# Second FFN of a fused attention and FFN kernel: SyncE's transfers in written order, token loads behind the last reads of their buffers, partial sums loaded two blocks ahead

## The chip, the core and the metric

One NeuronCore of a Trainium2 chip runs the whole program. Its engines work side by side, each in order: TensorE (PE) multiplies, VectorE (DVE), ScalarE (ACT) and GpSimd (POOL) work on tiles, SyncE (SP) issues most DMA transfers, ScalarE some. The metric is the device time of one execution in microseconds; the median of three runs is compared.

## What is computed

State attention, a first gated FFN (moe) and a second one (moe2). The change lies in the second, on 4352 tokens of 512 numbers (8 x 544), with 1536 hidden numbers:

```python
def _moe2_ref(x, w_gate, w_val, w_out):
    gate = 1.0 / (1.0 + np.exp(-(x @ w_gate)))
    val = x @ w_val
    return (gate * val @ w_out).astype(np.float32)
```

The weights arrive as 64-bit numbers. The kernel keeps each factor as a pair of rounded parts, high and low, and multiplies high with high, high with low and low with high.

## The kernel before, the second FFN

The 34 blocks of 128 tokens are cut in five groups, `c` = 0 to 4, of 7, 7, 7, 7 and 6 blocks. The 1536 hidden columns are cut in three passes, `ps`. So there are 15 steps `(ps, c)`, the passes outside. A step has two halves, `gate_val(ps, c, q, ...)` with q = 0 and 1, each for 256 hidden columns of the gate (a = 0) and of the value (a = 1). A half forms its 2 x 2 blocks of output (hidden by tokens, n = 448 or 384 tokens) by seven products of the Strassen-Winograd kind and not by eight: fourteen "products" of six matmuls for a = 0 and 1 together. They go to PSUM banks psA (k = 1, 6, 5, 3), psB (k = 7, 4) and psC (k = 2). psA is one running sum: after k = 1, 6 and 5 ScalarE copies it out (`keep_`, the rows u<-psA and s<-psA), and the next product into that bank waits for the copy. VectorE's `finish` adds and multiplies, ScalarE takes the sigmoid, and the result, split in two parts, is the tile p.

`down(ps, c)` multiplies p with the output weights, block by block, 12 matmuls of 512 columns each, into one of three po banks. It is put into the next step, behind the first three products of its first half (`between`). In the first pass the block is copied to a tile `ob` (VectorE and ScalarE by turns) and stored to `part_d[0]`; in the second and third pass the earlier partial sum is loaded to a tile `pr`, VectorE adds (line 1026), and the sum is stored to `part_d[1]` or the output. `pr` and `ob` have two buffers each; the load for block s + 1 is written in block s, ahead of its add.

Token tiles: the seven right-hand factors of group c + 1 ("tokens", tiles y) are made while group c is multiplied. `next_tokens` holds the list: four loads `get(kb, h)` of 448 KB (tile yf, three buffers; the fourth comes from ScalarE's queue), four sums per kb (`diff`, tiles yt), and fourteen `part`s, each a copy on ScalarE and a subtraction on VectorE (line 590, one step later). The fourth load of a group takes the buffer of its second, which is read early; the loads (0,1) and (1,0) of the next group wait for the very last reads of this group, the parts (5,1) and (6,1), which fall into the down.

Meanwhile `next_weights` makes the weights of the next pass: loads and stores on ScalarE's queue (`raw2`, `wd`), bit operations on ScalarE and VectorE (`conv`), sums on GpSimd (`comb`), splits on ScalarE and GpSimd (`put`). `load_wt(ps, q)` loads the two weight tiles `wt[q, 0]` and `wt[q, 1]` of a half, 1792 KB each; `load_wo` the output weights.

Order: within `tc.manual_schedule` ScalarE, VectorE and GpSimd run what the code writes, in that order. TensorE's order is written too. SyncE is not in the list: its transfers are placed by the tile framework's scheduler. A planner decides where tokens and weights stand: `clock` counts steps (a product 1.2 us, half a down block 1.35 us) and a budget of VectorE time; `begin` runs what is due (`later`), and `fill`, behind each product or each half block, takes list entries from `prep` and `tokens` while the entry's condition holds. `at(k)` is true k products behind the middle of a step. For the first entries, parts (0,0) and (0,1) and the first four sums, the condition is `begun`, three products behind the three loads, which stand together at the head of the step.

## Time and profile before

| | us |
|---|---|
| median of 3 runs | 1444.26 (1442.82 to 1445.51) |
| the profiled execution | 1441.65 |
| its span | 1439.8 |
| TensorE busy in the span | 1350.2 (94%) |
| VectorE, ScalarE, GpSimd busy | 958.2 (67%), 747.9 (52%), 279.8 (19%) |
| the second FFN's matmuls, first start to last end | 630.40 to 1431.02 |

From 630 us on TensorE is busy in nine tenths or more of nearly every slice of the page, and its granted clock reads 9 tenths or more in each. Its matmuls are pipelined, so the starts of groups that follow each other tell more than the busy time: where the next group starts later than the work before it takes, TensorE has lost time. The profile's "idle before" names who released it.

### The profile page before, as it was taken

The page shows a single profiled execution, that of the slowest core. Times are in us where ns is not written, and L with a number is a line of the kernel's source. Part 1 is how long each engine was busy: PE and PEld are TensorE (multiplying, and loading weights), DVE is VectorE, ACT ScalarE, POOL GpSimd, SP SyncE. Part 2 cuts the span into 40 slices and gives each one's busy share as a digit, 9 for nine tenths or more (in the row PEclk, how much of TensorE's full clock was granted, in tenths as well). Part 3 has the DMA queues.
Part 4 walks back from the last instruction along what each step waited for, and adds up shares of the span by engine and source line. Part 5 has one row for each costly group of instructions (what it writes and reads, how often), then busy time and mean ns, then how long its engine had stood idle before and what let it go on. Part 6 is the DMA issues. An engine that isn't in the chain of part 4 may idle for free. (4 is left out here: it accounts for less than half of the span.)

```text
span 1439.8 us, 19119 instructions
## 1 busy us (share of the span) xinstructions
PE 1350.2 (94%) x6560; PEld 1148.4 (80%) x6560; DVE 958.2 (67%) x1639; ACT 747.9 (52%) x1480; POOL 279.8 (19%) x255
## 2 busy tenths in 40 slices
PE   4667999999999999999999999899999999999997
PEld 3446877778777777898888998888978988988996
DVE  7789866664574575628578687678768557556543
ACT  6766557665455456535556555545545434434421
POOL 2253023323243234001122210221211000000000
PEclk9699999999999999999999999999999999999999
DMA  9767836764345244383343358464463662242232
GB/s 276 241 184 206 231 112 209 223 210 116 138 137 159 90 147 157 122 330 114 134 160 115 135 183 313 162 214 143 163 209 122 249 241 92 88 128 87 74 103 73
DMA packets 169129, 237.19 MB, mean 165 GB/s; under 512 B 46920, under 2 KB 111944, under 8 KB 166984
## 3 DMA queue, kind: packets, MB, share of 16 engines
q1 hardware_dynamic: 130536, 163.15, 36.2%
q10 hardware_dynamic: 37344, 63.39, 12.5%
q0 software_dynamic: 1152, 9.44, 1.7%
q8 instruction: 51, 0.84, 0.2%
q14 instruction: 46, 0.38, 0.1%
HBM read 150.99 MB, written 84.93 MB: 164 GB/s over the span
## 5 line engine op out<-in xcount | busy, mean ns | idle before, releaser
L912 PE MATMUL psA<-y,wt 128*128 128x448 f32 (+1 forms) x1440 | 307.9, 362 | 12.2 <-ACT u L61 11.7
L912 PEld LDWEIGHTS psA<-y,wt 128*128 128x128 f32 x1440 | 268.1, 189 | 34.1 <-ACT u L61 14.9
L1010 PE MATMUL po<-wo,p 128*128 128x512 f32 x1224 | 283.6, 392 | 4.2 <-DVE ob L1026 3.8
L1010 PEld LDWEIGHTS po<-wo,p 128*128 128x128 f32 x1224 | 229.9, 189 | 54.2 <-DVE ob L1026 5.5
L112 PE MATMUL pab<-aT,swh 128*128 128x512 f32 x512 | 146.1, 408 | 21.4 <-ACT asb L61 9.8
L912 PE MATMUL psB<-y,wt 128*128 128x448 f32 (+1 forms) x720 | 161.6, 360 | 0.0
L912 PEld LDWEIGHTS psB<-y,wt 128*128 128x128 f32 x720 | 134.2, 189 | 8.6
L66 POOL TENSOR_TENSOR o<-m,o 128x256 fp32r<-128x256 f32 x72 | 61.4, 853 | 384.6 <-ACT o L61 362.4
L112 PE MATMUL py<-u,wp 128*128 128x512 f32 (+1 forms) x576 | 131.6, 380 | 2.3 <-DVE u L66 2.0
L112 PEld LDWEIGHTS pab<-aT,swh 128*128 128x128 f32 x512 | 95.2, 193 | 45.2 <-ACT asb L61 11.6
L112 PEld LDWEIGHTS py<-u,wp 128*128 128x128 f32 x576 | 103.4, 188 | 28.4 <-issue 5.7
L61 ACT ACTIVATE u<-psA 128x448 f32<-128x448 f32 (+1 forms) x120 | 63.4, 529 | 118.2 <-PE psA L912 96.3
L66 POOL TENSOR_TENSOR swh<-swf,swh 128x512 fp32r<-128x512 f32 x64 | 93.4, 1463 | 159.3 <-ACT swh L61 132.1
L434 DVE TENSOR_TENSOR asb<-asb,pab 128x512 f32<-128x512 f32 (+1 forms) x72 | 47.1, 653 | 97.1 <-PE pab L115 90.2
L61 ACT ACTIVATE p<-sg 128x448 fp32r<-128x448 f32 (+1 forms) x120 | 67.9, 565 | 82.1 <-DVE sg L948 72.8
L61 ACT ACTIVATE y<-yf 128x448 fp32r<-128x448 f32 (+1 forms) x120 | 62.7, 557 | 69.9 <-DMA yf<-yd 67.3
L590 DVE TENSOR_TENSOR y<-yf,y 128x448 fp32r<-128x448 f32 (+1 forms) x112 | 67.5, 626 | 45.8 <-ACT y L61 45.8
L1026 DVE TENSOR_TENSOR ob<-po,pr 128x512 f32<-128x512 f32 x68 | 46.7, 687 | 59.8 <-DMA pr<-part 36.2
L98 DVE SCALAR_TENSOR_TENSOR m<-raw,m 128x512 uint32<-128x512 uint32 (+1 forms) x116 | 81.7, 706 | 2.8
L101 DVE CUSTOM_DVE_ANT_0 m<-m,r 128x1024 uint16<-128x1024 uint16 (+1 forms) x116 | 75.1, 648 | 10.3 <-ACT u L61 0.5
L115 PE MATMUL pab<-aT,swh 128*128 128x512 f32 x256 | 81.4, 400 | 0.2
L93 DVE TENSOR_SCALAR m<-m 128x512 f32<-128x512 f32 (+1 forms) x116 | 53.0, 457 | 42.9 <-ACT m L88 42.5
(119 smaller groups left out, 2090.8 us busy)
## 6 DMA issues: line engine op xcount, KB each, us to landing
raw<-in_moe_w SPq DMA_DIRECT2D x48, 512.0 KB, 5.0
wt<-wd SPq DMA_DIRECT2D x12, 1792.0 KB, 7.4
part<-ob SPq DMA_DIRECT2D x68, 256.0 KB, 2.8
pr<-part SPq DMA_DIRECT2D x68, 256.0 KB, 3.7
yf<-yd SPq DMA_DIRECT2D x37, 448.0 KB, 4.3
swd<-swst ACTq DMA_DIRECT2D x32, 512.0 KB, 3.6
swf<-swd SPq DMA_DIRECT2D x128, 128.0 KB, 3.3
wd<-o ACTq DMA_DIRECT2D x56, 256.0 KB, 2.3
```

The lines of the kernel that those rows point to most:

```text
L61: return nc.scalar.activation(out=o, in_=i, func=AF.Copy)
L66: (sub or nc.vector).tensor_tensor(out=lo, in0=src, in1=hi.bitcast(F32), op=ALU.subtract)
L93: nc.vector.tensor_scalar_max(m, m, 2.0**-15)
L98: nc.vector.scalar_tensor_tensor(out=mu, in0=hi, scalar=0xC0000000, in1=mu, op0=ALU.bitwise_and, op1=ALU.bitwise_or)
L101: nc.vector.tensor_tensor(out=m.bitcast(I32), in0=m.bitcast(I32), in1=r, op=ALU.add)
L112: nc.tensor.matmul(o, w[i], xx[k], start=n == 0 and i + k == 0, stop=False)
L115: nc.tensor.matmul(o, w[1 - late], xx[late], start=False, stop=n == len(pairs) - 1)
L434: p2["dve"] = nc.vector.tensor_tensor(out=asb[:, :n], in0=asb[:, :n], in1=pab[1][:, :n], op=ALU.mult)
L590: nc.vector.tensor_tensor(out=o, in0=x0, in1=x1, op=ALU.subtract)
L912: nc.tensor.matmul(o, w[:, i, kb * P : (kb + 1) * P], xx[kb][h], start=start, stop=i == 1 and kb == 1, skip_group_check=True,)
L1010: nc.tensor.matmul(o, pt[j][i][:, s * P : (s + 1) * P], wot[j][:, h], start=j == js[0] and i + h == 0, stop=j == js[-1] and i == 1,)
L1026: nc.vector.tensor_tensor(out=ob, in0=o, in1=pr[s], op=ALU.add)
```

## The change

1. SyncE joins the engines whose order is written. The transfers are therefore placed by hand: at the stage's head wt of the first half, the token loads, wt of the second half, the output weights; at a pass change `wt[1, 0]` before the down and `wt[1, 1]` behind it.
2. Of the three SyncE token loads only (0,0) stays at the head of a step; (0,1) and (1,0) become list entries behind part (6,1) of the group before, run one step later. `get` notes when a load should have landed by the planner (2.5 us plus 2.2 us each, one after the other); the first parts and sums wait for that (`here`). Part (0,1) now stands behind the four sums.
3. `load_pr` asks for block s + 2, two blocks ahead of the add; blocks 0 and 1 are asked for at the head of the step. `ob` and `pr` become one tile with four buffers, and the add is in place.
4. In `next_weights` a sum no longer stands in the same or the next entry to the split that reads it.

```diff
--- before.py
+++ after.py
@@ -668,7 +668,7 @@
 
 
 
-        clock = {"now": 0, "us": 0.0, "vector": 0.0, "prep": 10.0}
+        clock = {"now": 0, "us": 0.0, "vector": 0.0, "prep": 10.0, "load": 0.0}
         due = {}
         tokens = []
         prep = []
@@ -705,6 +705,9 @@
                         fn()
             while tokens and clock["vector"] > 0.5 and act < 2 and tokens[0][0]():
                 _, is_split, fn = tokens.pop(0)
+                if is_split is None:
+                    later(1, 0.0, fn)
+                    continue
                 if is_split:
                     act += 1
                 else:
@@ -718,8 +721,8 @@
         def new_p(j):
             pt[j] = [c2.tile([P, 896], F32R, name=f"p{j % JQ}_{i}") for i in range(2)]
 
-        def load_wt(ps, q):
-            for a in range(2):
+        def load_wt(ps, q, both=(0, 1)):
+            for a in both:
                 t = c2.tile([P, 7, 2, 256], F32R, name=f"wt{q}{a}")
                 nc.sync.dma_start(
                     out=t.rearrange("p o i f -> p (o i f)").bitcast(F32),
@@ -746,9 +749,11 @@
             ready.difference_update([(c, o, kb) for o in range(7) for kb in range(2)])
             raw = {}
             t = {}
+            landed = {}
 
             def get(kb, h, queue=nc.sync):
                 raw[kb, h] = y_raw(c, kb, h, c2, 448, queue)
+                clock["load"] = landed[kb, h] = max(clock["load"], clock["us"] + 2.5) + 2.2
 
             def diffs(kb):
                 (b11, b12), (b21, b22) = raw[kb, 0], raw[kb, 1]
@@ -777,13 +782,21 @@
                         later(2, 0.0, lambda: get(1, 1, nc.scalar))
                 return fn
 
+            def here(*need):
+                return lambda: all(k in landed and clock["us"] >= landed[k] for k in need)
+
             get(0, 0)
-            get(0, 1)
-            get(1, 0)
-            begun = clock["now"] + 3
-            first = at(1) if clock["now"] == 0 else lambda: clock["now"] > begun
-            out = [(first, True, part(0, 0)), (first, True, part(0, 1))]
-            out += [(first, False, lambda i=i: diff(0, i)) for i in range(4)]
+            if clock["now"] == 0:
+                get(0, 1)
+                get(1, 0)
+                first = [at(1)] * 3
+                out = []
+            else:
+                first = [here((0, 0)), here((0, 0), (0, 1)), here((1, 0))]
+                out = [(lambda: True, None, lambda k=k: get(*k)) for k in ((0, 1), (1, 0))]
+            out += [(first[0], True, part(0, 0))]
+            out += [(first[1], False, lambda i=i: diff(0, i)) for i in range(4)]
+            out += [(first[2], True, part(0, 1))]
             out += [(at(2), True, part(o, 0)) for o in (4, 5)]
             out += [(at(5), True, part(1, 0)), (at(8), True, part(4, 1))]
             out += [(at(8), True, part(o, 0)) for o in (2, 3)]
@@ -859,23 +872,20 @@
                     m["s"] = m[22]
 
                 def s2():
-                    put(d[5], 21)
+                    comb(21, 11, 21)
                     comb("s", "s", 11)
-
-                def s4():
-                    put(d[0], 11)
-                    comb("s", 12, "s")
 
                 get(21)
                 get(22)
                 step(s1)
+                get(11)
                 step(lambda: put(d[3], "s"))
-                get(11)
-                step(lambda: comb(21, 11, 21))
                 step(s2)
+                step(lambda: put(d[0], 11))
+                step(lambda: put(d[5], 21))
+                get(12)
                 step(lambda: put(d[4], "s"))
-                get(12)
-                step(s4)
+                step(lambda: comb("s", 12, "s"))
                 step(lambda: put(d[1], 12))
                 step(lambda: put(d[6], "s"))
 
@@ -991,16 +1001,15 @@
             ):
                 step(a, k)
 
+        pr = {}
+
+        def load_pr(ps, c, s):
+            if ps and s < blocks[c]:
+                pr[s] = c2.tile([P, DM], F32, name="ob", bufs=4)
+                nc.sync.dma_start(out=pr[s], in_=part_d[ps - 1][first[c] + s])
+
         def down(ps, c):
             js = range(ps * JQ, (ps + 1) * JQ)
-            pr = {}
-
-            def load_pr(s):
-                pr[s] = c2.tile([P, DM], F32, name="pr", bufs=2)
-                nc.sync.dma_start(out=pr[s], in_=part_d[ps - 1][first[c] + s])
-
-            if ps:
-                load_pr(0)
             for s in range(blocks[c]):
                 o = ps2.tile([P, DM], F32, tag="o", name="po", bufs=3)
                 for j in js:
@@ -1016,14 +1025,13 @@
                         )
                     if j % 2:
                         fill(True)
-                if ps and s + 1 < blocks[c]:
-                    load_pr(s + 1)
-                ob = c2.tile([P, DM], F32, name="ob", bufs=2)
+                load_pr(ps, c, s + 2)
                 g = first[c] + s
+                ob = pr.pop(s) if ps else c2.tile([P, DM], F32, name="ob", bufs=4)
                 if ps == 0:
                     copy("act" if s % 2 else "dve", ob, o)
                 else:
-                    nc.vector.tensor_tensor(out=ob, in0=o, in1=pr[s], op=ALU.add)
+                    nc.vector.tensor_tensor(out=ob, in0=o, in1=ob, op=ALU.add)
                 vector(0.69)
                 if ps < NPASS - 1:
                     nc.sync.dma_start(out=part_d[ps][g], in_=ob)
@@ -1039,16 +1047,19 @@
         for j in range(JQ):
             new_p(j)
         for name, n, w in (
-            ("ob", 2, DM), ("pr", 2, DM), ("sg00", 1, 448), ("sg01", 1, 448), ("sg10", 1, 448),
+            ("ob", 4, DM), ("sg00", 1, 448), ("sg01", 1, 448), ("sg10", 1, 448),
             ("sg11", 1, 448), ("raw2", 2, 512), ("o2", 2, 512), ("m2", 3, 256), ("r2", 1, 256),
             ("s1", 2, 448), ("u2", 2, 448), ("u4", 1, 448),
         ):
             c2.tile([P, w], F32, name=name, bufs=n)
         load_wt(0, 0)
-        load_wo(0)
-        load_wt(0, 1)
         steps = [(ps, c) for ps in range(NPASS) for c in range(NPAIR)]
-        ordered = {mybir.EngineType.Activation, mybir.EngineType.DVE, mybir.EngineType.Pool}
+        ordered = {
+            mybir.EngineType.Activation,
+            mybir.EngineType.DVE,
+            mybir.EngineType.Pool,
+            mybir.EngineType.SP,
+        }
         with tc.manual_schedule(engines=ordered):
             for i, (ps, c) in enumerate(steps):
                 if c == 0 and ps + 1 < NPASS:
@@ -1060,9 +1071,20 @@
 
                     tokens += next_tokens(steps[i + 1][1], at)
 
+                if i == 0:
+                    load_wt(0, 1)
+                    load_wo(0)
+                elif c == 0:
+                    load_wt(ps, 1, (0,))
+
+                for s in range(2 if i else 0):
+                    load_pr(*steps[i - 1], s)
+
                 def between():
                     if i:
                         down(*steps[i - 1])
+                        if c == 0:
+                            load_wt(ps, 1, (1,))
 
                 gate_val(ps, c, 0, between)
                 if c == NPAIR - 1 and ps + 1 < NPASS:
@@ -1074,7 +1096,8 @@
                 gate_val(ps, c, 1, lambda: None)
                 if c == NPAIR - 1 and ps + 1 < NPASS:
                     assert len(prep) < clock["out"] - 2, (len(prep), clock["out"])
-                    load_wt(ps + 1, 1)
+            for s in range(2):
+                load_pr(*steps[-1], s)
             for _ in range(3):
                 begin(0.0)
             down(*steps[-1])
```

At site A of the sections below, the first pass's first down (block 4 to the first two products behind it), ScalarE's order. y0<-yf is the copy of a `part`, o2 and wd belong to the weights, ob is a down block's eviction, u2<-psA the copy that frees the bank. Before:

```order
L61 ACTIVATE y0_6490<-yf_6007 128x448
L61 ACTIVATE y0_6493<-yf_6332 128x448
L61 ACTIVATE o2_6504<-m2_6176 128x256
L61 ACTIVATE y0_6508<-yf_6336 128x448
L819 DMA wd_64<-o2_6504 128x512
L61 ACTIVATE o2_6534<-m2_6367 128x256
L61 ACTIVATE ob_6539<-po_6514 128x512
L819 DMA wd_64<-o2_6534 128x512
L88 ACTIVATE m2_6556<-raw2_6391 128x256
L89 ACTIVATE r2_6557<-raw2_6391 128x256
L61 ACTIVATE u2_6577<-psA_6339 128x448
```

After:

```order
L61 ACTIVATE o2_6524<-m2_6177 128x256
L61 ACTIVATE ob_6527<-po_6510 128x512
L832 DMA wd_64<-o2_6524 128x512
L88 ACTIVATE m2_6544<-raw2_6386 128x256
L89 ACTIVATE r2_6545<-raw2_6386 128x256
L61 ACTIVATE u2_6570<-psA_6334 128x448
L817 DMA raw2_6578<-in_moe2_w_val 128x2x256
L61 ACTIVATE o2_6580<-m2_6362 128x256
L61 ACTIVATE u2_6585<-psA_6345 128x448
L61 ACTIVATE y0_6594<-yf_6495 128x448
```

The copy of part (0,1) of the next group (y0_6508, now y0_6594), which reads its third load, moved from ahead of the ob eviction to behind both u2 copies.

VectorE at the same place. y1 is the subtraction of a part, yt and the write to yf are the four sums, ob_6511/ob_6507 and ob_6560/ob_6552 the copies of blocks 4 and 6, the m2 rows the bit operations of a weight. Before:

```order
L590 TENSOR_TENSOR y1_6491<-yf_6007,y0_6490 128x448
L590 TENSOR_TENSOR y1_6494<-yf_6332,y0_6493 128x448
L62 COPY ob_6511<-po_6482 128x512
L590 TENSOR_TENSOR y1_6509<-yf_6336,y0_6508 128x448
L590 TENSOR_TENSOR yt_6522<-yf_6332 128x448
L590 TENSOR_TENSOR yt_6523<-yf_6334,yt_6522 128x448
L590 TENSOR_TENSOR yt_6524<-yf_6334,yf_6332 128x448
L590 TENSOR_TENSOR yf_6332<-yf_6334,yt_6523 128x448
L62 COPY ob_6560<-po_6542 128x512
```

After:

```order
L590 TENSOR_TENSOR y1_6487<-yf_5994,y0_6486 128x448
L590 TENSOR_TENSOR y1_6490<-yf_6331,y0_6489 128x448
L62 COPY ob_6507<-po_6478 128x512
L590 TENSOR_TENSOR yt_6548<-yf_6331 128x448
L62 COPY ob_6552<-po_6530 128x512
L93 TENSOR_SCALAR m2_6544<-m2_6544 128x256
L94 TENSOR_SCALAR m2_6544<-m2_6544 128x256
L98 SCALAR_TENSOR_TENSOR m2_6544<-raw2_6386,m2_6544 128x256
L101 ISA m2_6544<-m2_6544,r2_6545 128x512
L590 TENSOR_TENSOR yt_6549<-yf_6493,yt_6548 128x448
```

The first read of the second load (yf_6334, now yf_6493) moved behind block 6's copy and the four bit operations.

SyncE in the second pass, the down of group 1. pr, later ob, is the loaded partial sum, part1 the store, yf the token loads of group 3. Before:

```order
L584 DMA yf_9634<-yd3_62 128x896
L1029 DMA part1_67<-ob_9701 128x512
L1000 DMA pr_9725<-part0_66 128x512
L1029 DMA part1_67<-ob_9727 128x512
L1000 DMA pr_9759<-part0_66 128x512
L1029 DMA part1_67<-ob_9761 128x512
L584 DMA yf_9636<-yd3_62 128x896
L584 DMA yf_9638<-yd3_62 128x896
L1000 DMA pr_9791<-part0_66 128x512
L1029 DMA part1_67<-ob_9793 128x512
```

After:

```order
L584 DMA yf_9550<-yd3_62 128x896
L1009 DMA ob_9552<-part0_66 128x512
L1009 DMA ob_9554<-part0_66 128x512
L1009 DMA ob_9616<-part0_66 128x512
L1037 DMA part1_67<-ob_9552 128x512
L1009 DMA ob_9647<-part0_66 128x512
L1037 DMA part1_67<-ob_9554 128x512
L1009 DMA ob_9679<-part0_66 128x512
L1037 DMA part1_67<-ob_9616 128x512
L584 DMA yf_9684<-yd3_62 128x896
L584 DMA yf_9686<-yd3_62 128x896
L1009 DMA ob_9705<-part0_66 128x512
```

Where a store and one load took turns, three loads now stand ahead of the first store.

## Rows read from the trace of the kernel before

**Rows 1.** Groups by shape: line, engine, names, shapes, count | busy us, mean ns | idle before.

```profile
L912 PE MATMUL psA<-y,wt 128*128 128x448 f32 x1152 | 253.4, 369 | 12.0 <-ACT u L61 11.5 <-DVE sg L948 0.3
...
L912 PE MATMUL psA<-y,wt 128*128 128x384 f32 x288 | 54.5, 336 | 0.2 <-ACT u L61 0.2
...
L1010 PE MATMUL po<-wo,p 128*128 128x512 f32 x1224 | 283.6, 392 | 4.2 <-DVE ob L1026 3.8 <-DVE p L590 0.4
```

**Rows 2.** Chain that ended last, in order of time: start us, us, what.

```profile
1173.59 2.43 PE psA L912 x12
...
1368.81 19.08 PE po L1010 x84
...
1391.04 2.08 PE psA L912 x12
...
1416.19 14.83 PE po L1010 x64
```

**Rows 3.** TensorE's timeline: start us, us, engine, line, operation [idle before <-releaser].

```profile
630.40 2.60 PE L912 MATMUL psA<-y,wt 128*128 128x448 f32 x12
...
687.25 2.60 PE L912 MATMUL psA<-y,wt 128*128 128x448 f32 x12
...
699.69 1.58 PE L912 MATMUL psA<-y,wt 128*128 128x448 f32 x7
...
872.22 2.51 PE L912 MATMUL psA<-y,wt 128*128 128x384 f32 x12
...
882.46 1.78 PE L1010 MATMUL po<-wo,p 128*128 128x512 f32 x7
...
901.24 1.38 PE L912 MATMUL psB<-y,wt 128*128 128x448 f32 x6
...
910.67 1.38 PE L912 MATMUL psB<-y,wt 128*128 128x448 f32 x6
...
960.13 1.38 PE L912 MATMUL psB<-y,wt 128*128 128x448 f32 x6
...
966.14 1.38 PE L912 MATMUL psB<-y,wt 128*128 128x448 f32 x6
...
1068.73 1.38 PE L912 MATMUL psB<-y,wt 128*128 128x448 f32 x6
...
1075.35 1.38 PE L912 MATMUL psB<-y,wt 128*128 128x448 f32 x6
...
1152.86 13.76 PE L1010 MATMUL po<-wo,p 128*128 128x512 f32 x60
...
1173.39 2.63 PE L912 MATMUL psA<-y,wt 128*128 128x448 f32 x12
```

**Rows 4.** Waits of the whole span: engine line <- releaser: us, times, longest us.

```profile
ACT y L61 <- DMA yf<-yd: 67.3, 16, 7.2
...
DVE ob L1026 <- DMA pr<-part: 36.2, 17, 4.5
```

**Rows 5.** ScalarE's timeline at two of the sites.

```profile
688.39 0.58 ACT L61 ACTIVATE y<-yf 128x448 fp32r<-128x448 f32 x1 [5.49 <-DMA yf<-yd]
...
691.29 0.53 ACT L61 ACTIVATE u<-psA 128x448 f32<-128x448 f32 x1
...
874.88 0.58 ACT L61 ACTIVATE y<-yf 128x448 fp32r<-128x448 f32 x1 [0.23 <-DMA yf<-yd]
```

**Rows 6.** SyncE's timeline at the first site.

```profile
682.10 1.03 SPq L584 DMA_DIRECT2D yf<-yd  x2
```

**Rows 7.** VectorE's timeline at the first site.

```profile
682.16 1.16 DVE L590 TENSOR_TENSOR y<-yf,y 128x448 fp32r<-128x448 f32 x2 [0.22 <-ACT y L61]
```

**Rows 8.** Token loads (yf) from 660 to 1340 us: time from issue to landing.

```profile
DMA to landing us min/median/max: 2.9/4.1/8.9
```

**Rows 9.** Weight tile loads (wt, line 724): time from issue to landing.

```profile
DMA to landing us min/median/max: 6.9/7.4/10.9
```

**Rows 10.** DMA issues on the page: names, count, KB each, median us to landing.

```profile
pr<-part SPq DMA_DIRECT2D x68, 256.0 KB, 3.7
```

## The prediction

> **What bounds the kernel now.** I read the instruction groups by shape first, then the chain that ended last, then TensorE's own timeline in the second FFN, and only at TensorE's gaps the timelines of ScalarE, VectorE and SyncE. Each product of that FFN goes to psA four times, to psB twice and to psC once in seven (the table OPS), so 1152 psA matmuls of 448 columns stand for 2016 of that width, and 288 of 384 columns for 504; 1224 matmuls are the down projection's [rows 1]. Undisturbed, twelve 448-wide ones take 2.43 us, twelve 384-wide ones 2.08, and 84 of the down projection 19.08 [rows 2]. The work is 2016 x 0.2025 + 504 x 0.1733 + 1224 x 0.2271 = 408.2 + 87.4 + 278.0 = 773.6 us. The stage's first matmul starts at 630.40 [rows 3] and its last ends at 1416.19 + 14.83 = 1431.02 [rows 2]: 800.6 us. So TensorE loses **27.0 us** here. It works in order and is the only engine without long rests, so a microsecond taken from this loss is a microsecond of the kernel; nothing else that the change touches lies on the path.
>
> **Where the 27.0 us are.** The first and last row of each site stand in [rows 3]; the work between them at the prices above is taken off.
> - A, 687.25 to 699.69, 36 matmuls of 448: 12.44 - 7.29 = 5.1.
> - B, 901.24 to 910.67, 18 of them: 9.43 - 3.65 = 5.8.
> - C, 960.13 to 966.14, 18: 6.01 - 3.65 = 2.4.
> - D, 1068.73 to 1075.35, 18: 6.62 - 3.65 = 3.0.
> - F, 1152.86 to 1173.39, 72 of the down projection: 20.53 - 16.35 = 4.2.
> - H, 872.22 to 882.46, 30 of 384 and 18 of 448: 10.24 - 8.85 = 1.4.
>
> A, B, C, D and F make 20.5; with H it is 21.9, and 5.1 lie in pieces under 1 us each, most of them in the downs of the last pass. All five big sites lie at the end of a down or right behind one.
>
> **What makes them.** At A, VectorE reads the old tokens for the last time up to 683.3 [rows 7]; SyncE, which waits for these reads, issues the two loads between 682.10 and 683.1 [rows 6]; ScalarE already stands at the split that reads the second of them and waits 5.49 us, until 688.39 [rows 5]. What is written behind it on ScalarE waits too, first a down block's eviction, then the copy u<-psA that frees the bank for TensorE: it starts at 691.29 [rows 5], though its product was done near 688.5. Over the kernel ScalarE waited 67.3 us in 16 such places, and VectorE 36.2 us in 17 places for the partial sums' loads [rows 4]. The transfers aren't slow, they are asked for too late, or used too early.
>
> **The change part by part.**
> *Token loads and their readers.* The loads can't start sooner: the buffers are the same three, so they still wait for the same last readers. What moves is who reads. Of the first reads, that of the third load stands behind both copies u<-psA (the first pair of fences), and VectorE's first read of the second load behind the last block's ob copy and the four bit operations of a weight, some 0.4 us each (the second pair). At A, by the times of before: the last block ends at 687.25, a copy of 0.68 us and 1.5 us of bit operations bring VectorE to the load at 689.4, and ScalarE comes to its split behind the second copy, after the two products that end at 689.7, near 690.2. The loads landed for the read at 688.39. Cover left: 1.0 and 1.8 us, so A goes whole. In the last pass no weights are converted; VectorE comes to the load four half blocks (5.5 us) and one subtraction behind the place of its issue, which is about its landing time (median 4.1, longest 8.9 [rows 8]); what is late there meets three po banks, so 0 to 1 us per pair. The splits written later still end before TensorE's next pair needs them: the next readers in the list keep their places in the second half.
>
> *Partial sums two blocks ahead.* The load is issued beside the add of block s-1 for block s+1 now, and lands in a median of 3.7 us [rows 10] where one block is 12 x 0.2271 = 2.7: it has 5.5 us less SyncE's own issues, which fails whenever SyncE is held. Changed, block s+2 is asked for before the store of block s, three blocks or 8.2 us ahead less the wait for the store of s-2; the first two start at the head of the step, three products earlier. The 36.2 us of VectorE go nearly whole. They are worth little by themselves (VectorE has rests), but they are half of what makes F and the last pass's pieces. Four ob buffers in the place of two ob and two pr take the same room, and adding in place costs nothing.
>
> *SyncE in written order.* No transfer is added. First weights: wt for the second half comes behind the three token loads; it is needed fourteen products (17 us) after the stage begins and takes 7.4 us: nothing. At a pass change one of the four weight tiles, wt[1,1], is issued only behind the down's sixth store; twelve products pass before its first reader, 14.6 us, against 7.4 and at most 10.9 [rows 9]: hidden, with 3.7 us to spare for SyncE itself being held.
>
> *Weight preparation reordered on GpSimd and ScalarE.* Same operations; a sum now stands one step or more ahead of its split. 0, and if the cover is gone, some tenths at few places.
>
> **Sum.** A, B, C, D and F go: 20.5. H stays, since its load comes on ScalarE's queue among two weight tiles as before (the split at 874.88 waits for it [rows 5]). Of the 5.1 of small pieces I take half, 2.6: those in downs go, those in the second halves stay. New waits: bounds 0 and 13 pairs x 0.5 = 6.5; I take 1.4, near the lower end, because A's covers are positive. Gain 20.5 + 2.6 - 1.4 = 21.7 us. The profiled execution, 1441.65, would come to 1420.0; it lies 2.6 under the median of the runs, so against 1444.26 I forecast **1422.6 us**.
>
> **One rule against it.** The rows show weight tiles that need 6.9 to 10.9 us [rows 9] and small loads that need up to 8.9 [rows 8], without saying what stood before what. The Trainium skill ("DMA: Bandwidth & Descriptors", "Queues, rings and completion order") says that an engine takes the descriptors of one queue in ring order, so that on SyncE's queue a small load behind a weight tile waits for its bytes; the written order puts partial sums right behind a weight tile at the second pass change. No row of this trace tells the two apart. By the rows' medians the sum stays as it is; by ring order it is the third rival.
>
> **The rivals.**
> 1. *The wait moves along.* VectorE takes ScalarE's place: its first read comes before the landing, and its adds hold the po banks. For it: SyncE still waits for the same readers. Against: the cover above, and that VectorE's next task for TensorE has three banks of slack. If half of the 23.1 stays: 1444.3 - 11.5 = 1432.7. Chance 0.17.
> 2. *It doesn't do what it says*: the loads are bounded by the last reads alone, every wait only changes its name. 1444 within 2.9 us. Against: [rows 5] show that the held instruction is what costs, and it is moved. Chance 0.07.
> 3. *Behind the weight tile.* The two first partial sums of the second pass change wait for 10.9 us of weights and then 3.7 of their own; issued near 1149 they land near 1163.6, and block 3 can't start at 1152.86 + 8.2 = 1161.0 [rows 3] until the add of block 0 is through, 0.7 later. One stall of 3.2 us: 1425.8. Chance 0.10, nearly all inside my own range.
> 4. *Slower: ScalarE's late split inside the products.* The split of the third load now stands among the copies u<-psA and those of the next products. A copy has two products, 2.4 us, until TensorE needs its bank again. With 13 pairs, the kernel is slower by over 2.9 us if each loses (21.7 + 2.9) / 13 = 1.9 us more, that is if the load lands 4.3 us after ScalarE reaches the split; at A the split stands 7.1 us behind the issue (690.2 less 683.1), so the point is a landing of 11.4 us, against a longest of 8.9 [rows 8]. 1447 and more. Chance 0.06.
>
> **How the numbers follow.** Forecast as summed, 0.60, its own range 1419 to 1428 (from all 27.0 but H and the end, to the upper bound of new waits). Rivals 1 to 4: 0.17, 0.07, 0.10, 0.06. The range 1418 to 1434 holds the forecast, the third rival and most of the first, about 0.82. Within 0.2% is 2.9 us, about what a measurement of this kernel can tell from no change. Faster by more: 0.60 + 0.17 + 0.10 = 0.87, less 0.01 for the first rival's tail, so 0.86; within 0.2%: 0.08; slower: 0.06.
>
> **What would show it.** In the changed profile: waits of ScalarE for yf far under 67 us and of VectorE for partial sums near 0; no gap of TensorE over 1 us at the end of a down but at H; the stage from first to last matmul near 779 us. Wrong would be: a gap in the products behind a down with ScalarE's y split before it (rival 4), VectorE's yt rows held by yf and po matmuls held by ob (rival 1), po held near block 3 of the second pass change (rival 3), or matmuls held by nothing but a weight tile behind a pass change.

## The result, and the profile after

In five runs each the changed kernel took 1426.32 us in the median (1425.04 to 1429.27) and the kernel before 1445.51 (1442.82 to 1452.37): ratio 0.9863, 95% interval 0.9834 to 0.9891, 19.2 us less. The forecast was 1422.6, with 1418 to 1434 as the range.

The answers to [rows 2, 3]: first and last group of the stage in TensorE's timeline after the change (start us, us, engine, line, operation [idle before <-releaser]).

```profile
633.28 2.60 PE L922 MATMUL psA<-y,wt 128*128 128x448 f32 x12
...
1403.51 14.79 PE L1019 MATMUL po<-wo,p 128*128 128x512 f32 x64 [0.41 <-DVE p L590]
```

The stage lasts 1403.51 + 14.79 - 633.28 = 785.0 us: 15.6 less than before, where 779 was forecast. The profiled execution (1429.27) is the slowest of its five, and its stage begins 2.9 us later than before's, behind code that the change doesn't touch. Over all the profiles of this study it began between 629.9 and 634.4, so below kernels are compared by the stage's length too (first start to last end of its matmuls); the changed kernel, profiled twice, gave 785.0 and 783.6.

Groups by shape, answering [rows 1], and waits of the whole span, answering [rows 4].

```profile
L1019 PE MATMUL po<-wo,p 128*128 128x512 f32 x1224 | 280.7, 389 | 0.4 <-DVE p L590 0.4
L922 PE MATMUL psA<-y,wt 128*128 128x448 f32 x1152 | 251.5, 367 | 5.1 <-ACT sg L947 2.5 <-ACT u L61 1.4 <-DVE sg L958 1.2
```

```profile
ACT y L61 <- DMA yf<-yd: 31.5, 13, 7.4
...
DVE ob L1034 <- DMA ob<-part: 2.4, 2, 1.6
```

TensorE no longer waits for the add of a partial sum (3.8 us before), and 1.4 us for u copies in the place of 11.5. ScalarE's 67.3 us fell to 31.5, of which 20.7 are three waits in the last pass that hold nobody. What is new is `sg`: 2.5 us of waits that the kernel before didn't have. With 773.6 us of work, 11.4 us are lost, in few places. The largest is the second pass change:

```profile
1137.46 1.20 PE L922 MATMUL psB<-y,wt 128*128 128x384 f32 x6
1140.57 1.49 PE L922 MATMUL psA<-y,wt 128*128 128x448 f32 x6 [1.90 <-ACT sg L947]
1142.65 2.53 PE L922 MATMUL psA<-y,wt 128*128 128x448 f32 x6 [0.59 <-DVE sg L958]
1144.97 1.94 PE L922 MATMUL psC<-y,wt 128*128 128x448 f32 x6
1146.75 16.50 PE L1019 MATMUL po<-wo,p 128*128 128x512 f32 x72
```

From the last product of the old pass to the down's start is 6 x 0.1733 + 18 x 0.2025 = 4.7 us of work; it took 9.3, so 4.6 were lost. The same stretch of the first pass change, 874.69 to 881.87, lost 2.5. Before, the first change lost 1.1 and the second 0.8. ScalarE's timeline shows why (ACTq is its queue's issue):

```profile
1128.88 0.33 ACTq L817 DMA_DIRECT2D raw<-in_moe_w_out  x1
1130.47 0.33 ACTq L584 DMA_DIRECT2D yf<-yd  x1
...
1136.83 0.42 ACT L61 ACTIVATE o<-m 128x256 fp32r<-128x256 f32 x1 [2.46 <-DMA wod<-o]
1138.63 0.58 ACT L61 ACTIVATE y<-yf 128x448 fp32r<-128x448 f32 x1 [1.39 <-DMA yf<-yd]
...
1140.04 0.47 ACT L947 ACTIVATE sg<-psA 128x384 f32<-128x384 f32 x1
```

The fourth token load is asked for at 1130.47, right behind a raw load of 256 KB, and its first reader starts 8.2 us later; the sigmoid that empties psA stands behind that reader. The load is not alone: a split `o` of the weights, ahead of its reader, had waited 2.46 us for a store. Without the load's 1.39 TensorE would still have waited about 0.5 us of its 1.90 (an estimate from these rows). The chain of waits has the load as one piece of 8.14 us:

```profile
1130.47 8.14 DMA yf<-yd
...
1138.63 0.58 ACT y L61
```

The second place is near 955 us, 1.6 us lost. SyncE asked for the last partial sum only behind two token loads; VectorE's add waited for it, the weight's bit operations behind that add were late, ScalarE's split `o` waited for those (3.11 us), and the u copy stood behind that split.

```profile
945.89 1.32 SPq L584 DMA_DIRECT2D yf<-yd  x2
947.25 0.51 SPq L1009 DMA_DIRECT2D ob<-part  x1
```

```profile
954.23 0.69 DVE L1034 TENSOR_TENSOR ob<-po,ob 128x512 f32<-128x512 f32 x1 [1.60 <-DMA ob<-part]
```

```profile
957.79 1.50 PE L922 MATMUL psA<-y,wt 128*128 128x448 f32 x6 [1.40 <-ACT u L61]
```

### The profile page after: what moved, and what is told of

Same layout as the page of the kernel before. It is cut to its first block, busy times and chain, and to the rows that moved or that the text cites. A ratio compares the mean times of both kernels' runs of the same rounds, so it can differ in the third digit from the quotient of the medians.

```text
span 1427.5 us, 19086 instructions
## 1 busy us (share of the span) xinstructions
PE 1348.3 (94%) x6560; PEld 1148.6 (80%) x6560; DVE 966.6 (68%) x1639; ACT 749.1 (52%) x1480; POOL 282.2 (20%) x255
## 4 chain that ended last, share of the span: by engine, by line
PE 73%; DVE 5%; DMA 3%; issue 2%; ACT 2%; POOL 0%; SPq 0%; ACTq 0%; DVEq 0%; POOLq 0%
PE po L1019 18%; PE psA L922 18%; PE psB L922 9%; PE pab L112 7%; PE py L112 7%; PE psC L922 5%; PE pab L115 4%; PE py L115 3%; DMA yf<-yd 1%; DVE y L590 1%; DMA raw<-in_moe_w 1%; PE pxt L170 1%; PE psr L245 1%; PE psc L186 1%; PE psw L112 1%
## 5 line engine op out<-in xcount | busy, mean ns | idle before, releaser
L1019 PE MATMUL po<-wo,p 128*128 128x512 f32 x1224 | 280.7, 389 | 0.4 <-DVE p L590 0.4
L1034 DVE TENSOR_TENSOR ob<-po,ob 128x512 f32<-128x512 f32 x68 | 46.7, 687 | 56.2 <-PE po L1019 52.1
L922 PE MATMUL psC<-y,wt 128*128 128x448 f32 (+1 forms) x360 | 81.4, 362 | 1.0 <-DVE s L955 1.0
L66 DVE TENSOR_TENSOR u<-asb,u 128x512 fp32r<-128x512 f32 (+1 forms) x72 | 59.8, 831 | 30.9 <-ACT u L61 30.7
L88 ACT ACTIVATE m<-raw 128x512 f32<-128x512 f32 (+1 forms) x116 | 65.9, 568 | 28.2 <-POOL o L66 14.9
```

The costliest lines, as they stand in the source:

```text
L66: (sub or nc.vector).tensor_tensor(out=lo, in0=src, in1=hi.bitcast(F32), op=ALU.subtract)
L88: nc.scalar.activation(out=m, in_=hi.bitcast(F32), func=AF.Abs)
L922: nc.tensor.matmul(o, w[:, i, kb * P : (kb + 1) * P], xx[kb][h], start=start, stop=i == 1 and kb == 1, skip_group_check=True,)
L1019: nc.tensor.matmul(o, pt[j][i][:, s * P : (s + 1) * P], wot[j][:, h], start=j == js[0] and i + h == 0, stop=j == js[-1] and i == 1,)
L1034: nc.vector.tensor_tensor(out=ob, in0=o, in1=ob, op=ALU.add)
```

## The experiments

Each stands against the kernel before on its own chip (ratio), and by its stage. "Pass changes" is the loss in the two stretches, first and second, measured as above. A stage is that of one profiled execution. That of the kernel before is 3.9 us faster than its median, that of the changed kernel 3.0 slower, and e11's, 6.0 us under its median, is the fastest of its twelve runs. Where a stage and a ratio disagree, the ratio says more.

| kernel | median us | ratio, 95% interval | stage us | pass changes us |
|---|---|---|---|---|
| before | 1445.51 | 1 | 800.6 | 1.1 + 0.8 |
| changed | 1426.32 | 0.9863 (0.9834 to 0.9891) | 785.0 | 2.5 + 4.6 |
| e9, changed again | 1426.24 | 0.9884 (0.9860 to 0.9908) | 783.6 | 4.3 + 2.7 |
| e7, late reads alone | 1426.58 | 0.9872 (0.9854 to 0.9889) | 783.6 | 1.2 + 0.7 |
| e1, early reads | 1455.06 | 1.0076 (1.0057 to 1.0095) | 811.1 | 1.6 + 2.6 |
| e11, e1 and SyncE placed | 1444.71 | 1.0005 (0.9985 to 1.0026) | 796.7 | 2.3 + 2.1 |
| e2, one block ahead | 1431.62 | 0.9910 (0.9890 to 0.9930) | 789.0 | 1.7 + 2.2 |
| e3, SyncE placed | 1422.80 | 0.9846 (0.9829 to 0.9864) | 781.6 | 2.3 + 3.5 |
| e4, old sums | 1419.60 | 0.9827 (0.9811 to 0.9843) | 779.1 | 1.2 + 1.4 |
| e5, merged entry | 1428.88 | 0.9881 (0.9862 to 0.9900) | 787.5 | 1.2 + 0.7 |
| e6, e4 and SyncE placed | 1420.98 | 0.9828 (0.9807 to 0.9849) | 778.9 | 1.2 + 0.6 |
| e8, fourth load on SyncE | 1423.54 | 0.9851 (0.9831 to 0.9871) | 781.1 | 1.8 + 3.0 |
| e10, before, new sums | 1442.47 | 0.9995 (0.9980 to 1.0009) | 797.8 | 2.4 + 2.6 |
| e12, e4 and e8 | 1421.84 | 0.9850 (0.9823 to 0.9878) | 780.3 | 1.2 + 1.1 |

**The place of the readers: e1, e11, e7.**

```diff
-                return lambda: all(k in landed and clock["us"] >= landed[k] for k in need)
+                return lambda: clock["now"] > begun and all(k in landed for k in need)
...
+            out += [(first[2], True, part(0, 1))]
             out += [(first[1], False, lambda i=i: diff(0, i)) for i in range(4)]
-            out += [(first[2], True, part(0, 1))]
```

> The changed kernel with its loads and SyncE order kept, but the first readers of the loads (0,0), (0,1), (1,0) back in the old place: three steps behind the head of the step, part (0,1) ahead of the four sums. Theory (what costs is the reader that is written too early, not the load): ScalarE again stands at the split of the third load while it is under way and holds the copies that free psA; A, B, C and F come back, 17.5 us by the rows of before, less what the earlier partial sums spare at F (half of 4.2): some 12 to 18 us longer than the changed kernel, 1438 to 1444 us, stage 797 to 803 us, ScalarE's waits for yf above 55 us. Rival (the loads now start earlier since SyncE is no longer held by other transfers, and the readers' place is of no weight): within 3 us of the changed kernel, 1424 to 1429 us, and the splits' waits stay near 31 us.

The stage grew by 26.1 us and is 10.5 us longer than before the change: the theory's direction, beyond its bound. Waits of the whole span in e1, then VectorE at one of the downs, and TensorE behind it:

```profile
ACT y L61 <- DMA yf<-yd: 99.4, 18, 9.3
DVE yt L590 <- DMA yf<-yd: 34.5, 10, 5.1
```

```profile
1122.29 0.63 DVE L590 TENSOR_TENSOR yt<-yf,yt 128x448 f32<-128x448 f32 x1 [4.58 <-DMA yf<-yd]
```

```profile
1126.29 4.61 PE L1020 MATMUL po<-wo,p 128*128 128x512 f32 x12 [2.66 <-DVE ob L1035]
```

A sum that stands too early on VectorE holds the adds, and these the po banks. Whether the written order makes this worse, e11 asked: e1 with SyncE taken out of the list.

```diff
-            mybir.EngineType.SP,
```

> The edit of e1 (first readers back to the early place) and SyncE out of the written order. e1 took 811.1 us in the stage, 10.5 more than the kernel before. Theory A (the written order of SyncE makes an early reader worse, since the token loads stand behind stores and partial sums): the stage comes down to 800 to 805 us, 1443 to 1449 us. Theory B (the early readers alone are that costly, together with the new order of the sums): the stage stays at 808 to 814 us, 1451 to 1458 us.

By the two profiles 14.4 us came back, by the ratios (1.0076 to 1.0005) some 10; the stage is below theory A's range, the median inside it. Early readers are dear anyhow: against e3, which differs by the readers alone, 15.1 us by the stages (796.7 and 781.6) and 23 by the ratios. In a written order of SyncE, with the load behind stores and partial sums, they are dearer still, 26.1 by the stages. e7 then made the second part of the change alone in the kernel before (the diff's lines on `get`, `here` and `out`; the weight tiles written as in the change, SyncE placed by the framework).

> The kernel before with only the second part of the change: token loads (0,1) and (1,0) written behind the last parts, their first readers held back by the planner's landing times, part (0,1) behind the sums. SyncE is placed by the framework, partial sums are loaded one block ahead to pr, the weights' sums are in the old order. Theory (the late readers are the main part): A, B, C, D and F's ScalarE half go, the small pieces in the last pass stay: stage 782 to 787 us, 1422 to 1429 us. Rival (each part alone is worth little, since VectorE's adds wait for partial sums and the written SyncE order is needed for the loads' place): stage over 792 us, over 1434 us.

17.0 us of the stage: as much as the whole change brings.

**Partial sums: e2.**

```diff
-                load_pr(ps, c, s + 2)
+                load_pr(ps, c, s + 1)
...
-                ob = pr.pop(s) if ps else c2.tile([P, DM], F32, name="ob", bufs=4)
+                ob = c2.tile([P, DM], F32, name="ob", bufs=2)
```

> The changed kernel with the partial sums as before: a tile pr and a tile ob of two buffers each, the first load at the head of the down, block s+1 asked for in block s, the sum written to ob. SyncE stays in written order. Theory: the early loads spare F's half and the small pieces of the last pass, 2 to 5 us together: 1428 to 1432 us, VectorE's waits for partial sums back to 25 us or more, small gaps of TensorE in the downs of the last two passes. Rival (VectorE has rests, three po banks cover it): within 1.5 us of the changed kernel. Second rival (in written order the load for the next block stands behind token loads that wait for their last readers, so one block ahead is worse than it was): over 8 us longer, with po waiting for the add at each down from the second pass on.

4.0 us of the stage, as expected, but not where expected. VectorE waited 50.4 us for partial sums, more than before the change, and in the last pass no matmul waits for an add. The price is paid near 955 us, at the place shown above (6.5 us lost, 1.6 in the changed kernel; the pass changes lose 3.2 less), where the load (SyncE, VectorE, TensorE) stands behind two token loads:

```profile
944.46 1.28 SPq L584 DMA_DIRECT2D yf<-yd  x2
945.83 0.47 SPq L1009 DMA_DIRECT2D pr<-part  x1
```

```profile
952.42 0.69 DVE L1035 TENSOR_TENSOR ob<-po,pr 128x512 f32<-128x512 f32 x1 [6.73 <-DMA pr<-part]
```

```profile
958.97 2.60 PE L922 MATMUL psA<-y,wt 128*128 128x448 f32 x6 [4.08 <-ACT u L61]
```

From e7 to e6, which has the two loads ahead and four buffers too, it is 4.7 us. Most of that is paid in the first pass, which has no partial sums to load: with two `ob` buffers VectorE's copy of a block waits for a store there, in e7:

```profile
900.22 0.69 DVE L62 COPY ob<-po 128x512 f32<-128x512 f32 x1 [4.70 <-DMA part<-ob]
```

Behind that copy TensorE lost 3.9 us in e7 near 904 us; in e6 nothing is lost there. So these 4.7 us speak for the buffers more than for the early loads.

**SyncE's order: e3, e6.** e3 is the changed kernel with the one line of e11.

> The changed kernel with SyncE taken out of the written order again; all else kept. The framework then puts the four weight tiles of a pass change together ahead of the down, mixes the token loads with stores, and asks for partial sums earlier. Theory (the written order of SyncE is needed only so that the rest can be placed; what pays is the place of the readers): within 3 us of the changed kernel, 1423 to 1429 us. Rival (the written order is itself a large part of the gain, since a transfer that waits holds those behind it): 6 us or more longer, with waits for yf or partial sums that are not in the changed kernel.

3.4 us less against the first profile of the changed kernel, a little past the theory's 3, and 2.0 against the second. In e3 nothing is lost near 955 us. e6 is e4 with the same line:

> The edits of e3 and e4 together: the weights' sums in the old order and SyncE out of the written order; the late reads and the partial sums two blocks ahead stay. Theory (two separate costs, 3.4 and 5.9 us of the stage): stage 775.7, about 1416 us. Rival (both act at the pass changes and can be saved only once): stage 779 to 780, as e4, 1419 to 1421 us.

Its stage is e4's (778.9 and 779.1): the theory of two separate costs fell, the rival held. Once the readers stand late, nothing shows a gain from the written order.

**The sums of the weights: e4, e10, e5.** e4 puts back the `step` list of the kernel before.

```diff
-                    comb(21, 11, 21)
+                    put(d[5], 21)
                     comb("s", "s", 11)
...
+                def s4():
+                    put(d[0], 11)
+                    comb("s", 12, "s")
```

> The changed kernel with the weights' sums and splits in the old order (a sum in the entry of the split that reads it, or next to it). Theory A (the order on GpSimd and ScalarE costs nothing, and the stalls at the pass changes come from the fourth token load being slow among the weight tiles): stage within 1.5 us of 785.0, 1425 to 1428 us, and the stalls near 875 and 1137 us stay (2.4 and 4.6 us in the changed kernel). Theory B (the new order made the preparation later, so a raw load of 256 KB stands 1.6 us ahead of the fourth token load on ScalarE's queue at both pass changes): the load lands 1.5 to 3 us sooner, the stalls at the pass changes shrink by 2 to 4 us. Theory C (the old order made ScalarE wait for GpSimd): 3 us or more longer, waits of ScalarE's o rows for GpSimd above those of the changed kernel (7.3 us).

Theory B: 5.9 us (4.5 against the second profile of the changed kernel), and 4.5 of them at the pass changes. Of these 0.8 are the lower clock that the last section shows, which e4's stage never has. The new list has one entry more for each of the four groups of a pass, 54 for the factors in the place of 50, so the output weights come later. In e4 no raw load is issued near the second pass change (the fourth token load's issue, then TensorE):

```profile
1124.08 0.33 ACTq L584 DMA_DIRECT2D yf<-yd  x1
...
1132.62 1.21 PE L925 MATMUL psB<-y,wt 128*128 128x384 f32 x6
1133.79 1.49 PE L925 MATMUL psA<-y,wt 128*128 128x448 f32 x6
1135.95 1.50 PE L925 MATMUL psA<-y,wt 128*128 128x448 f32 x6 [0.67 <-DVE sg L961]
```

Its fourth load landed in 5.0 and 7.3 us, against 6.8 and 8.1 in the changed kernel. At the second change it was also asked for earlier, 8.5 us ahead of the old pass's last product (1124.08 to 1132.62) and not 7.0 (1130.47 to 1137.46). e10 made the same edit the other way, in the kernel before.

> The kernel before with only the new order of the weights' sums and splits (54 and 16 entries a pass in the place of 50 and 16). Theory (the four entries push the preparation into the pass changes, and that costs some 5 us wherever the rest stands): stage 804 to 808 us against 800.6, 1448 to 1452 us, raw loads near the fourth token load at both pass changes and stalls there of 2 to 5 us (1.1 and 0.8 in the kernel before). Rival (it costs only where the late reads already stand close to the landing): stage 799 to 803 us, 1442 to 1447 us.

At the pass changes the theory held: 5.0 us in the place of 1.9. For the whole it fell, the stage is 2.8 us shorter and the time the same: the shifted preparation also left site B without a loss (5.8 before), while site C lost 3.6 (2.4 before). The stage is under both forecasts, the median in the rival's. Why B went is open. e5 kept the new order of the sums and saved the entries:

```diff
-                step(lambda: put(d[0], 11))
-                step(lambda: put(d[5], 21))
+                step(lambda: (put(d[0], 11), put(d[5], 21)))
```

> The changed kernel with one edit: the splits of 11 and of 21 in one entry of the preparation's list, so that a group has twelve and a half entries no more but the number of before (50 and 16 a pass, not 54 and 16). The sums still stand a step ahead of the splits that read them. In the planner's order the last output weight of the second pass is then split at 468, not at 530 us of its clock. Theory (lateness: four entries more push the preparation into the pass changes, where its loads stand ahead of the fourth token load): the 5.9 us that the old order brought in e4 are brought by this too, stage 778 to 781 us, 1418 to 1422 us, no raw load near the fourth token load at the second pass change. Rival (the order on GpSimd: a sum in its own entry holds ScalarE's splits and VectorE differently): the stage stays within 1.5 us of 785.0, 1424 to 1428 us.

By the total neither theory holds, by place lateness does: the pass changes fall to 1.2 + 0.7. But two splits in one entry need both `o2` buffers at once, and the next waits for a store (ScalarE, then TensorE):

```profile
912.67 0.42 ACT L61 ACTIVATE o<-m 128x256 fp32r<-128x256 f32 x1 [6.08 <-DMA wd<-o]
```

```profile
916.28 4.85 PE L921 MATMUL psA<-y,wt 128*128 128x448 f32 x12 [4.27 <-ACT s L61]
```

That one stall, with what follows it, costs 7.1 us. Over the table, the six profiles with the shorter list (before, e4 to e7, e12) lose 1.8 to 2.6 us at the pass changes, and the eight with the longer one 3.9 to 7.1 (two of them, the changed kernel and e9, with some 0.8 of lower clock in it).

**The fourth load's queue: e8, e12.**

```diff
-                        later(2, 0.0, lambda: get(1, 1, nc.scalar))
+                        later(2, 0.0, lambda: get(1, 1))
```

> The changed kernel with the fourth token load issued by SyncE, behind the two weight tiles of a pass change, and not by ScalarE behind a raw load. Theory A (the raw load of 256 KB in rows of 512 B ahead of it on ScalarE's queue is what makes it late): it lands in 4 to 6 us and not in 6.8 and 8.2, the stalls at the two pass changes (2.4 and 4.6 us) shrink to 1.5 and 2; stage 781 to 783. Theory B (the engines are full of weight tiles, whatever the queue; on SyncE's queue it even stands behind their bytes): it lands no sooner than 6.8 us, stalls as large or larger by up to 2 us each, stage 784 to 789. Either way SyncE may be held by it at other steps, where no transfer stands behind it until the next step's head.

Between the two: it landed in 6.1 and 7.4 us, 0.7 sooner each, and 2.3 us came back at the pass changes, 0.8 of them because the clock didn't fall there. But the unedited kernel's landings differ by as much from one profile to the next (6.8 and 8.1, in e9 7.8 and 7.1), so a share of the raw load ahead of it is not shown. (That load's packets are of 2048 bytes in the trace, not of the 512 that the expectation has.) For the weight tiles as most of its time speak the traces' DMA packets: at the first change the fourth load's first packet starts at 871.2 us in the changed kernel and at 868.5 in e4, just when the last of the tiles' start (871.0 and 868.5); at the second it starts 0.9 and 2.2 us ahead of their last. With e4's list there should be no raw load to get past:

> The edits of e4 and e8 together: sums in the old order, the fourth token load from SyncE. Theory (e8's gain of 3.9 us came from getting past raw loads which in the old order aren't there): stage as e4, 778 to 780 us, 1418 to 1421 us. Rival (it is a second saving of its own): 776 us or less, under 1417 us.

The stage is e4's within 1.2 us, a little past the theory's 780; the rival's 776 is ruled out. **The best versions** are e4 and e6 (0.9827 and 0.9828), not told apart. e4's interval lies under that of the changed kernel run again (0.9860 to 0.9908) and touches that of its first runs (from 0.9834).

> The changed kernel once more, unedited, beside the next three on one chip. Stage 784 to 786 us, the stalls of 2.5 and 4.6 us at the two pass changes and of 1.6 us near 955 us in the same places if they are a matter of order, in other places if they are chance; 1424 to 1428 us.

The stalls stood in the same places, 7.0 us at the pass changes, but shared out the other way round (4.3 and 2.7), and 0.7 near 955: the places are a matter of order, the sizes vary. At the pass changes two things moved with the larger stall: the fourth load's landing (7.8 and 7.1 us here, 6.8 and 8.1 there) and the lower clock, some 0.8 us, at the first change here and at the second there.

## Why the forecast was right, point by point

- **Where the loss was, and the readers (A to D and half of F, 18.4 us).** Right in mechanism and nearly in size: A, B, D and F are gone from TensorE's timeline, and C is down to the 1.6 us near 955, with another cause. e7 alone gives 17.0, e3 against e11 15.1. One part of the mechanism was missed: behind the waits at A, B and F the granted clock had fallen, as the last section shows, so 5.0 of the 20.5 us were no waits. They went with the waits, so the sum did not suffer. The cover held: VectorE's sums waited 9.0 us for loads, 5 times, without holding a po bank. The loads themselves didn't get faster, as the answer to [rows 8] shows:

```profile
DMA to landing us min/median/max: 3.0/4.3/8.0
```

- **Partial sums, half of F and the small pieces in the last pass.** The size is right (4.0 to 4.7), the place was not, so the agreement is luck: the last pass needs late reads only, and the early loads pay where SyncE's queue holds a load behind token loads, and through the four buffers in the first pass.
- **SyncE in written order, nothing.** Right beside the old sums (e6 is as e4), but not of itself: in the changed kernel it costs 2.0 to 3.4 us of the stage (e3), where two profiles of one kernel differ by 1.4, and with early readers some 10 us by the ratios and 14.4 by the profiles. `wt[1,1]` was hidden: issued at 899.50, landed in 8.4 us.
- **Weight preparation, "0, and if the cover is gone, some tenths".** This is the step that failed. It measured 5.9 us here (4.5 against e9). In the kernel before the same edit cost 3.1 at the pass changes and nothing in all (e10). I compared operations and their order, and did not count the entries of a list that is worked off at a fixed spacing. "H stays" fell with it: the two pass changes lost 7.1 us where I had 1.4 and a small piece. Without this edit (e4) the stage is 779.1, the forecast's 779.
- **New waits, 1.4.** 1.6 near 955 us, by the mechanism of the first rival (VectorE waits, others stand behind it), at one place only. That the size agrees is in part luck, since e9 lost 0.7 there. The stalls at the pass changes bear the fourth rival's sign, a gap with ScalarE's y split before it, but at the fourth load, where the rival meant the third. The second rival is ruled out by e7, which moves the readers and shortens the stage by 17.0.
- **The third rival.** At the second pass change a weight tile was issued at 1144.03 and landed in 7.4 us, at 1151.4; the three partial sums issued behind it from 1144.51 landed in 7.6 to 8.0, the first at 1152.1. So they land on the tile's heels, against a median of 3.8 for such loads. The DMA packets of SyncE's queue have the same order: the tile's start from 1146.1 to 1150.4, the partial sums' from 1150.6. The rule of the Trainium skill that the prediction weighed ("DMA: Bandwidth & Descriptors", "Queues, rings and completion order") agrees with that. What failed of the rival was its sum: it laid 10.9 and 3.7 us end to end from a later issue, and three banks covered the rest, since the down's 72 matmuls run without a gap.
- **Why 1426.3 and not 1422.6.** By the medians 19.2 us came of the 21.7, by the stage 15.6 and 17.0. The mis-sized weights (4.5 to 5.9) cover either shortfall within the spread of two profiles of one kernel (785.0 and 783.6).

## What to carry to other kernels

A load that waits for a buffer can't be made earlier, but its first reader can be written later; hold it back by the time that the load should land, on every engine that reads it. Before you call a reordering free, count what it adds to a list that is worked off at a fixed pace, and look where its tail now ends. The rows near 955 us also suggest, on a queue in written order, to put a small urgent load ahead of a large one that must wait; no run here tested that alone.

## What was not expected of the hardware

In these traces a stall of TensorE can cost more than its length, since in or behind some rests its granted clock fell. Stretches of time (start:end, us, then busy us and instructions of PE, PEld, DVE, ACT and POOL, then the granted clock, DMA share and GB/s): first in e5, during and behind the rest of 4.27 us.

```profile
912.00:916.20 4.20, 0.01 (x1) 0.00 (x0) 1.20 (x3) 2.32 (x5) 0.72 (x1) 0.87 0.36 133
916.30:920.90 4.60, 4.60 (x12) 4.11 (x13) 4.29 (x10) 3.80 (x9) 0.14 (x1) 0.50 0.02 3
```

At 0.50, the lower level of 1.2 GHz, twelve matmuls took 4.65 us to the next group's start and not 2.43: 2.2 us on top of the wait. In the changed kernel the same twelve matmuls stand at both pass changes:

```profile
878.60:881.87 3.27, 2.82 (x12) 2.28 (x13) 3.24 (x7) 1.79 (x4) 0.00 (x0) 1.00 0.38 95
...
1142.70:1146.70 4.00, 4.00 (x12) 3.58 (x13) 3.86 (x9) 1.93 (x4) 0.00 (x0) 0.57 0.53 179
```

At 1.00 they took 3.27 us with a wait of 0.45 among them; at the second change, behind the waits of 1.90 and 0.59 us, they took 4.10 (1142.65 to 1146.75). So some 0.8 of the 4.6 us lost there are the clock's. In the kernel before, the ends of A, B and F, behind their waits:

```profile
695.57:699.69 4.12, 4.12 (x13) 3.70 (x14) 0.62 (x1) 2.16 (x5) 1.76 (x4) 0.59 0.50 179
906.58:910.67 4.09, 4.09 (x12) 3.58 (x13) 0.49 (x1) 2.03 (x5) 1.43 (x2) 0.58 1.00 371
1168.98:1173.39 4.41, 4.41 (x12) 3.46 (x13) 2.40 (x4) 0.00 (x0) 0.00 (x0) 0.62 0.75 236
```

Each has twelve matmuls to work off, of 2.43, 2.43 and 2.73 us undisturbed, so each lost 1.7 us to the clock. The page, in slices of 36 us, reads 9 tenths there all the same. Not every rest does this. In e10 TensorE waited 3.27 us for a u copy up to 964.25, and the twelve matmuls behind it ran in 2.53 us at 1.00:

```profile
964.25:966.78 2.53, 2.53 (x12) 2.36 (x13) 0.62 (x1) 1.00 (x3) 1.10 (x2) 1.00 0.66 230
```

What decides it, these runs don't show.
